# Half two's differences of x formed in PSUM, the last layer's group sums staged later, the third matrix and y in pieces of 384, 384 and 256 columns

## The chip, the core and the metric

One core of a Trainium2 chip runs the whole program. Its engines are TensorE (PE, whose weight loads the profile lists as PEld), VectorE (DVE), ScalarE (ACT), GpSimd (POOL) and SyncE (SP, which here only issues transfers). Each takes its instructions in the order in which they were written. The metric is the device time of one execution in microseconds (us), the median of three runs.

## The reference

Attention whose heads are mixed before and after the softmax, then two layers of matrix products without biases, all in fp32, over 1792 tokens (4 sequences of 448):

```python
scores = np.einsum('bhij,hg->bgij', scale * q @ k^T, w_pre)
attn   = softmax(scores)
attn   = np.einsum('bhij,hg->bgij', attn, w_post)
x = (attn @ v) as [1792, 768]
h = (x @ w1) * (x @ w2)            # [1792, 1024]
x = (h @ w3) @ w_out               # [1792, 768]
h = np.maximum(x @ w_in, 0.0)      # [1792, 2048]
out = (h * h) @ w_out2             # [1792, 768]
```

## The kernel before

**Products.** Every fp32 product is made of three matmuls (`mm3`, its matmul is line 62): each operand is split into a rounded high part and the rest, and the products high·high, high·low and low·high add up in one PSUM bank. A split costs two instructions: a copy on ACT that makes the high part, and a subtraction on DVE or POOL that makes the low part. Weights are split where they are used, and so is x.

**Order.** The class `Moe` holds a list of units, and each unit is a list of weight pieces (one piece is one step). `stage(s)` writes what step s needs ahead: the load of a piece six steps ahead on SP's queue; four ahead the narrowing on ACT (line 95), which with two DVE instructions three ahead (lines 106 and 108, called a join here) turns a fetched piece into fp32; three ahead the high part on ACT (line 122); two ahead the low part on POOL (line 164). Then the step's own matmuls are written. `lead` moves a piece's staging earlier by so many steps. Since all engines work in the order written, one instruction that comes late holds back what stands behind it on its engine.

**The third matrix.** w3 @ w_out is formed on the chip: eight units `p34` write it to a buffer in DRAM, `w34d`, from which the units `ly` read it back to form y. Both take 1024 columns of weights per unit, in four pieces of 256: step i does one of two accumulators (t = i mod 2) for half of the columns, so that its step 0 takes pieces 0 and 1, and step 2 takes pieces 2 and 3. Steps named in `free` also carry a job `side`, which rewrites a part of w_in into fp32 (a transfer in, ACT, DVE, a transfer out).

**Two halves.** Tokens are worked in two halves, each of two blocks of 448 columns. For half two, layers three and four save an eighth of the matmuls: a 2 by 2 block product is made of seven, which need sums of weights (S1 to S4, `combine`, DVE, line 160) and differences of the other operand: T1 = B12 − B11, T2 = B22 − T1, T3 = B22 − B12, T4 = B21 − T2. For x of half two these come from `quad_x`, called once per unit u of the last two phases of half one's fourth layer (`l4_part`, six units of two steps each per phase). It serves column blocks 1, 0 and 2, from units 4, 6 and 8 on: `chain` forms the four differences in SBUF on DVE, one unit later T2, T1, T3 and T4 are split (`split`; ACT makes the high parts, DVE the low parts of T2 and T3, POOL those of T1 and T4), and one unit after that B11, B21 and B22 (POOL, DVE, POOL). The phases' sums themselves are added up on DVE by `add` (line 832), from PSUM accumulators named `l`.

**The last layer.** `l4_group` makes four groups of 21 pieces, which add into banks named `l_` + group + p + X, Y or Z. A bank is read by `add` when a sum is whole, and then used again for another sum. The list `order` takes the products 1, 5, 6, 3, 7, 2, 4; pieces 8 and 9 are the ones with S3.

**PSUM.** All eight banks are one ring (tag "m"): a new tile takes the bank of the eighth tile before it and waits until that has been read.

Of the kernel before, what the change touches and what calls it, by code (L numbers as in the profile page):

```python
# [13 lines left out]
AF = mybir.ActivationFunctionType  # L14
# [24 lines left out]
def fused_kernel(ctx, tc, q, k, v, w_pre, w_post, w1, w2, w3t, wo, win, wo2, eye, out):  # L39
# [510 lines left out]
    class Moe:  # L550
        def __init__(self, pre):
# [6 lines left out]
            for hf in range(2):  # L558
# [21 lines left out]
                if hf == 0:  # L580
                    k = self.turned
                    self.free = {(i, t) for i in (*range(self.p34_at, k - 4), *range(k, k + 4)) for t in (1, 3)}
                    self.free |= {(i, 1) for i in range(k - 4, k)}
                    self.free |= {(k + 9 + e, 0) for e in range(6)}
                    self.free |= {(k + 17, 0)}
# [12 lines left out]
            for u in range(self.turned, len(self.units)):  # L598
                n, quad = len(self.units[u][0]), self.pieces[self.at[u]][0] is None
                for i in range(n if quad else 0):  # L600
                    self.lead[self.at[u] + i] = (4 if i < 6 else 3) if n > 7 and i < 8 else 2 if u > self.turned + 6 else 1
            self.keep = {
# [183 lines left out]
        def quad_x(self, u):  # L786
# [23 lines left out]
            def chain(c):  # L810
                spare("T3", c)
                spare("T4", c)
                for out, x, y in (
                    ("T3", "B22", "B12"), ("T1", "B12", "B11"), ("T2", "B22", "T1"), ("T4", "B21", "T2"),
                ):
                    x, y = (b["raw", n] if n[0] == "T" else f32(b["T1" if n == "B12" else n, c][1]) for n in (x, y))
                    t = b["raw", out] = self.tile(f"{out}raw{c}")
                    nc.vector.tensor_tensor(t, x, y, ALU.subtract)

            V, G = nc.vector, nc.gpsimd  # L820
            for c, at in ((1, 4), (0, 6), (2, 8)):
                if u == at:
                    chain(c)
                if u == at + 1:
                    for name, eng in (("T2", V), ("T1", G), ("T3", V), ("T4", G)):
                        split(name, c, eng)
                if u == at + 2:
                    for name, eng in (("B11", G), ("B21", V), ("B22", G)):
                        split(name, c, eng)

# [224 lines left out]
        def p34(self, m):  # L1055
            acc = {}

            def run(ws, i):
                part, t = divmod(i, 2)
                if part == 0:  # L1060
                    acc[t] = self.psum(f"p34_{m}_{t}")[:, :HC]
                mm3(acc[t], [(self.chunk(ws, c), self.wot[c, t]) for c in range(4 * part, 4 * part + 4)], part == 0, part == 1)
                if part == 0:
                    return
                o = self.tile(f"o34_{m}_{t}")[:, :HC]
                nc.scalar.activation(o, acc[t], AF.Copy)
                nc.scalar.dma_start(
                    w34d[3 * t : 3 * t + 3, :, m].rearrange("n p c -> p n c"), o.rearrange("p (n c) -> p n c", c=128)
                )

            return [(w3t[m, :, QW * i : QW * i + QW], True) for i in range(4)], run

        def ly(self, hf, n):
            acc = {}

            def run(ws, i):
                part, t = divmod(i, 2)
                if hf and n == 0:
                    t = 1 - t
                if part == 0:  # L1080
                    acc[t] = self.psum(f"y{hf}_{n}_{t}")
                cs = range(4 * part, 4 * part + 4)
                mm3(acc[t], [(self.chunk(ws, c), self.xy["ab", hf, c, t]) for c in cs], part == 0, part == 1)
                if part:
                    self.yquad(hf, n, t, acc[t])

            src = w34d[n].rearrange("p c n -> p (c n)")
            return [(src[:, QW * i : QW * i + QW], False) for i in range(4)], run

# [215 lines left out]
```

## Time and profile before

| | |
|---|---|
| median of three runs | 1285.67 us (1285.01 to 1286.91) |
| the profiled execution | 1287.36 us, of which the span from the first to the last instruction is 1285.6 |
| busy: PE, DVE, ACT, POOL | 1245.3, 915.1, 777.6, 618.5 us (97%, 71%, 60%, 48%) |
| granted TensorE clock | 0.997 on average |
| PE instructions | 8326 matmuls |

The page of the profile gives each engine's busy time over the span. A window view gives the same for a stretch of it, with the granted clock and the share of time in which the transfer engines were busy. A wait view tells what released an engine and for how long it had waited, and a timeline lists the instructions of one engine in order, with the idle time ahead of each in brackets where there was some. Window views here are of the matmuls of line 62 alone. The stretches are: the third matrix from 536.32 us to 606.66, the last phase of half one's fourth layer with the first product of half two's third layer behind it from 851.50 to 918.47, and one group of the last layer from 1151.95 to 1178.43.

### The profile page before, as it was taken

The page shows a single profiled execution, that of the slowest core. Times are in us where ns is not written, and L with a number is a line of the kernel's source. Part 1 is how long each engine was busy: PE and PEld are TensorE (multiplying, and loading weights), DVE is VectorE, ACT ScalarE, POOL GpSimd, SP SyncE. Part 2 cuts the span into 40 slices and gives each one's busy share as a digit, 9 for nine tenths or more (in the row PEclk, how much of TensorE's full clock was granted, in tenths as well). Part 3 has the DMA queues.
Part 4 walks back from the last instruction along what each step waited for, and adds up shares of the span by engine and source line. Part 5 has one row for each costly group of instructions (what it writes and reads, how often), then busy time and mean ns, then how long its engine had stood idle before and what let it go on. Part 6 is the DMA issues. An engine that isn't in the chain of part 4 may idle for free. (4 is left out here: it accounts for less than half of the span.)

```text
span 1285.6 us, 24324 instructions
## 1 busy us (share of the span) xinstructions
PE 1245.3 (97%) x8326; PEld 1070.0 (83%) x8326; DVE 915.1 (71%) x1756; ACT 777.6 (60%) x1808; POOL 618.5 (48%) x736
## 2 busy tenths in 40 slices
PE   7999999999998999999999999999899999999998
PEld 3677777777775788998999999999799999899897
DVE  4888899788877966665555867579767424666957
ACT  5988889888887754554455755455333344653543
POOL 4354255246322622333366443536765464855845
PEclk9999999999999999999999999999999999999999
DMA  6666476566555757699755576485421116235042
GB/s 216 169 176 200 130 198 215 138 175 189 175 156 169 213 180 216 189 272 297 246 160 173 185 249 204 150 268 166 150 74 50 46 59 198 64 122 183 15 154 86
DMA packets 138577, 214.48 MB, mean 167 GB/s; under 512 B 25301, under 2 KB 106197, under 8 KB 137941
## 3 DMA queue, kind: packets, MB, share of 16 engines
q1 hardware_dynamic: 114576, 190.30, 48.4%
q10 hardware_dynamic: 23877, 22.63, 5.1%
q8 instruction: 66, 1.08, 0.3%
q14 instruction: 58, 0.48, 0.1%
HBM read 128.73 MB, written 45.61 MB: 136 GB/s over the span
## 5 line engine op out<-in xcount | busy, mean ns | idle before, releaser
L164 POOL TENSOR_TENSOR wl<-f,wh 128x256 fp32r<-128x256 f32 (+1 forms) x112 | 97.9, 875 | 199.7 <-ACT wh L122 162.7
L338 PE MATMUL sp<-r,kpre 120*120 120x448 f32 x360 | 159.8, 565 | 11.3 <-ACT p L352 6.6
L352 ACT ACTIVATE p<-sp,nm 120x448 f32<-120x448 f32 x180 | 113.6, 642 | 50.3 <-DVE nm L344 50.2
L394 DVE SCALAR_TENSOR_TENSOR pl<-p,sm,ph 120x448 f16<-120x448 f32 (+3 forms) x270 | 137.9, 564 | 0.3 <-POOL ph L380 0.3
L344 DVE TENSOR_REDUCE nm<-sp 120x1 f32<-120x448 f32 x180 | 107.3, 617 | 42.5 <-PE sp L338 38.4
L367 POOL TENSOR_SCALAR sm<-sm 120x2 f32<-120x2 f32 (+3 forms) x94 | 24.6, 261 | 205.5 <-ACT p L352 201.1
L403 PEld LDWEIGHTS <-ph 120*128 120x128 f16 x1260 | 93.0, 98 | 32.6 <-issue 24.1
L378 ACT ACTIVATE ph<-p,sm 120x448 f16<-120x448 f32 (+1 forms) x180 | 107.8, 664 | 17.6 <-DVE sm L372 14.1
L403 PE MATMUL tp<-kwh,ph 120*128 120x120 f16 x630 | 106.1, 217 | 5.4 <-DVE p L419 2.4
L338 PEld LDWEIGHTS sp<-r,kpre 120*120 120x120 f32 x360 | 58.9, 184 | 55.7 <-issue 21.1
L403 PE MATMUL tp<-kwh,pl 120*128 120x120 f16 x630 | 105.2, 216 | 0.0
L403 PE MATMUL tp<-kwl,ph 120*128 120x120 f16 x630 | 105.2, 216 | 0.0
L312 PE MATMUL sc<-kt,qh 128*110 128x448 f32 (+1 forms) x192 | 99.4, 518 | 2.0 <-DVE kt L276 1.3
L323 ACT ACTIVATE s<-sc 110x448 f32<-110x448 f32 (+1 forms) x186 | 90.5, 559 | 7.6 <-PE sc L312 6.8
L122 ACT ACTIVATE wh<-f 128x256 fp32r<-128x256 f32 (+1 forms) x112 | 49.8, 444 | 73.0 <-DVE f L108 70.2
L164 POOL TENSOR_TENSOR wl<-quadh,wh 128x384 fp32r<-128x384 f32 x48 | 51.3, 1072 | 72.7 <-ACT wh L122 53.7
L95 ACT ACTIVATE y<-raw 128x256 f32<-128x256 f32 (+1 forms) x128 | 60.2, 473 | 39.4 <-DMA raw<-w3t 16.4
L455 PE MATMUL pv<-p,v 128*64 128x110 f32 (+1 forms) x1536 | 81.0, 262 | 0.6 <-ACT xs L465 0.6
L455 PEld LDWEIGHTS pv<-p,v 128*64 128x64 f32 x1536 | 74.1, 137 | 4.0 <-ACT xs L465 0.9
L417 DVE TENSOR_SCALAR p<-tp,iv 128x360 f32<-128x360 f32 x135 | 74.2, 577 | 1.3 <-PE tp L403 1.3
L106 DVE TENSOR_SCALAR f<-y 128x256 int32<-128x256 int32 (+1 forms) x128 | 58.8, 459 | 21.3 <-ACT y L95 21.2
L108 DVE SCALAR_TENSOR_TENSOR f<-raw,f 128x256 int32<-128x256 int32 (+1 forms) x128 | 68.2, 533 | 4.4
(3093 smaller groups left out, 3936.5 us busy)
## 6 DMA issues: line engine op xcount, KB each, us to landing
r<-s SPq DMA_DIRECT2D x172, 210.0 KB
raw<-w SPq DMA_DIRECT2D x32, 384.0 KB
sraw<-win SPq DMA_DIRECT2D x32, 384.0 KB
raw<-wo SPq DMA_DIRECT2D x48, 256.0 KB
kraw<-k SPq DMA_DIRECT2D x24, 448.0 KB
quadh<-wind SPq DMA_DIRECT2D x24, 384.0 KB
raw<-w3t SPq DMA_DIRECT2D x32, 256.0 KB
qraw<-q SPq DMA_DIRECT2D x35, 220.0 KB
```

The lines of the kernel that those rows point to most:

```text
L108: nc.vector.scalar_tensor_tensor(fi, raw[:, :, 0], 29, fi, ALU.logical_shift_right, ALU.bitwise_or)
L164: eng.tensor_tensor(self.out[i][1], self.ft.pop(i), f32(self.out[i][0]), ALU.subtract)
L312: nc.tensor.matmul(sc[:ic], t[:, hh * ic : hh * ic + ic], self.kt[b, h // 2][:, h % 2], start=(i == 0), stop=(i == 1))
L323: nc.scalar.activation(self.st[n][:ic, h], self.sc.pop((n, h))[:ic], AF.Copy)
L338: nc.tensor.matmul(t[:kk], self.kpre[:kk, :kk], self.rt.pop(g)[:kk], start=True, stop=True)
L344: nc.vector.tensor_reduce(nm[:kk], self.sp[g][:kk], AX.X, ALU.max, negate=True)
L352: nc.scalar.activation(p[:kk], self.sp.pop(g)[:kk], AF.Exp, bias=self.nm.pop(g)[:kk], accum_out=self.sm[g // 2][:kk, g % 2 : g % 2 + 1],)
L378: nc.scalar.activation(h[:, to], p[:, fr], AF.Copy, scale=sm)
L394: nc.vector.scalar_tensor_tensor(l[:, to], p[:, fr], sm, h[:, to], ALU.mult, ALU.subtract)
L403: nc.tensor.matmul(t[:, j], p[:, at : at + 128], w, start=(i == 0), stop=(i == 2))
L417: nc.vector.tensor_scalar(d, t[:, main], self.iv, None, ALU.mult)
L455: nc.tensor.matmul(t[64 * e : 64 * e + 64, x, :w], self.v[b][:, j, g], self.p2[n][:, j * NH + g, :w], start=(j == 0), stop=(j == JC - 1),)
```

## The change

Three things are rewritten.

1. In `quad_x`, ACT first copies B12 into a PSUM tile (`b12x`). DVE forms T1 in a second PSUM tile, T3 over the copy, and T2 in a third. One unit later (`fourth`) ACT makes T2's high part, DVE its low part, and DVE forms T4 over T2. Then T1, T3 and T4 are split with DVE making the low parts, and B11 and B22 with POOL; B21 follows a unit later on POOL. So each column block has eight DVE instructions instead of seven, all with an operand in PSUM, three on POOL instead of four, and eight on ACT instead of seven; and three tiles more go through the ring of PSUM banks.
2. In `l4_group`'s pieces, `lead` of pieces 8 and 9 falls from 2 to 0, and that of the later pieces from 2 to 1.
3. `p34` and `ly` take their 1024 columns in pieces of 384, 384 and 256; each step does both accumulators with the columns of its own piece alone. The `side` jobs stand at steps 0 and 1. The matmuls are the same in number; the pieces per unit are three instead of four, and their ACT, DVE and POOL instructions too.

```diff
                     k = self.turned
-                    self.free = {(i, t) for i in (*range(self.p34_at, k - 4), *range(k, k + 4)) for t in (1, 3)}
+                    self.free = {(i, t) for i in (*range(self.p34_at, k - 4), *range(k, k + 4)) for t in (0, 1)}
                     self.free |= {(i, 1) for i in range(k - 4, k)}
...
                 for i in range(n if quad else 0):
-                    self.lead[self.at[u] + i] = (4 if i < 6 else 3) if n > 7 and i < 8 else 2 if u > self.turned + 6 else 1
+                    self.lead[self.at[u] + i] = (4 if i < 6 else 3 if i < 8 else i > 9) if n > 7 else 2 if u > self.turned + 6 else 1
             self.keep = {
...
             def chain(c):
...
                 spare("T4", c)
-                for out, x, y in (
-                    ("T3", "B22", "B12"), ("T1", "B12", "B11"), ("T2", "B22", "T1"), ("T4", "B21", "T2"),
+                b12, t1, t2 = (self.psum(f"{n}x{c}") for n in ("b12", "t1", "t2"))
+                nc.scalar.activation(b12, f32(b["T1", c][1]), AF.Copy)
+                for out, t, x, y in (
+                    ("T1", t1, b12, "B11"), ("T3", b12, "B22", b12), ("T2", t2, "B22", t1),
                 ):
-                    x, y = (b["raw", n] if n[0] == "T" else f32(b["T1" if n == "B12" else n, c][1]) for n in (x, y))
-                    t = b["raw", out] = self.tile(f"{out}raw{c}")
-                    nc.vector.tensor_tensor(t, x, y, ALU.subtract)
+                    x, y = (f32(b[n, c][1]) if isinstance(n, str) else n for n in (x, y))
+                    b["raw", out] = t
+                    V.tensor_tensor(t, x, y, ALU.subtract)
+
+            def fourth(c):
+                h, l = b["T2", c]
+                t = b["raw", "T4"] = b.pop(("raw", "T2"))
+                nc.scalar.activation(h, t, AF.Copy)
+                V.tensor_tensor(l, t, f32(h), ALU.subtract)
+                V.tensor_tensor(t, f32(b["B21", c][1]), t, ALU.subtract)
 
...
                 if u == at + 1:
-                    for name, eng in (("T2", V), ("T1", G), ("T3", V), ("T4", G)):
-                        split(name, c, eng)
+                    fourth(c)
+                    for name in ("T1", "T3", "T4"):
+                        split(name, c, V)
+                    for name in ("B11", "B22"):
+                        split(name, c, G)
                 if u == at + 2:
-                    for name, eng in (("B11", G), ("B21", V), ("B22", G)):
-                        split(name, c, eng)
+                    split("B21", c, G)
 
         def add(self, out, x, y, eng=nc.vector):
...
             def run(ws, i):
-                part, t = divmod(i, 2)
-                if part == 0:
-                    acc[t] = self.psum(f"p34_{m}_{t}")[:, :HC]
-                mm3(acc[t], [(self.chunk(ws, c), self.wot[c, t]) for c in range(4 * part, 4 * part + 4)], part == 0, part == 1)
-                if part == 0:
-                    return
-                o = self.tile(f"o34_{m}_{t}")[:, :HC]
-                nc.scalar.activation(o, acc[t], AF.Copy)
-                nc.scalar.dma_start(
-                    w34d[3 * t : 3 * t + 3, :, m].rearrange("n p c -> p n c"), o.rearrange("p (n c) -> p n c", c=128)
-                )
-
-            return [(w3t[m, :, QW * i : QW * i + QW], True) for i in range(4)], run
+                for t in range(2):
+                    if i == 0:
+                        acc[t] = self.psum(f"p34_{m}_{t}")[:, :HC]
+                    cs = range(3 * i, min(3 * i + 3, 8))
+                    mm3(acc[t], [(self.chunk(ws, c), self.wot[c, t]) for c in cs], i == 0, i == 2)
+                    if i < 2:
+                        continue
+                    o = self.tile(f"o34_{m}_{t}")[:, :HC]
+                    nc.scalar.activation(o, acc[t], AF.Copy)
+                    nc.scalar.dma_start(
+                        w34d[3 * t : 3 * t + 3, :, m].rearrange("n p c -> p n c"), o.rearrange("p (n c) -> p n c", c=128)
+                    )
+
+            return [(w3t[m, :, HC * i : min(HC * i + HC, 1024)], True) for i in range(3)], run
 
         def ly(self, hf, n):
...
             def run(ws, i):
-                part, t = divmod(i, 2)
-                if hf and n == 0:
-                    t = 1 - t
-                if part == 0:
-                    acc[t] = self.psum(f"y{hf}_{n}_{t}")
-                cs = range(4 * part, 4 * part + 4)
-                mm3(acc[t], [(self.chunk(ws, c), self.xy["ab", hf, c, t]) for c in cs], part == 0, part == 1)
-                if part:
-                    self.yquad(hf, n, t, acc[t])
+                for t in (1, 0) if hf and n == 0 else (0, 1):
+                    if i == 0:
+                        acc[t] = self.psum(f"y{hf}_{n}_{t}")
+                    cs = range(3 * i, min(3 * i + 3, 8))
+                    mm3(acc[t], [(self.chunk(ws, c), self.xy["ab", hf, c, t]) for c in cs], i == 0, i == 2)
+                    if i == 2:
+                        self.yquad(hf, n, t, acc[t])
 
             src = w34d[n].rearrange("p c n -> p (c n)")
-            return [(src[:, QW * i : QW * i + QW], False) for i in range(4)], run
+            return [(src[:, HC * i : min(HC * i + HC, 1024)], False) for i in range(3)], run
 
         def side(self, k):
```

On DVE, in the second phase that serves x (column block 1, `f` and `y` are weight pieces, `l_2_4` an accumulator of the phase, `oa_4` its running sum, `x1l` blocks of x), before:

```order
L818 TENSOR_TENSOR T3raw_11920<-x1l_11747 128x448
L818 TENSOR_TENSOR T1raw_11922<-x1l_11747,x1l_11684 128x448
L818 TENSOR_TENSOR T2raw_11924<-x1l_11747,T1raw_11922 128x448
L818 TENSOR_TENSOR T4raw_11926<-x1l_11684,T2raw_11924 128x448
L106 TENSOR_SCALAR f_11948<-y_11908 128x256
L108 SCALAR_TENSOR_TENSOR f_11948<-raw_11854,f_11948 128x256
L832 TENSOR_TENSOR oa_4_1_10540<-l_2_4_1_11928,oa_4_1_10540 128x448
L832 TENSOR_TENSOR oa_4_0_10542<-l_2_4_0_11935,oa_4_0_10542 128x448
L106 TENSOR_SCALAR f_11974<-y_11946 128x256
L108 SCALAR_TENSOR_TENSOR f_11974<-raw_11880,f_11974 128x256
L804 TENSOR_TENSOR T21l<-T2raw_11924,T21h 128x448
L804 TENSOR_TENSOR T31l<-T3raw_11920,T31h 128x448
```

and after:

```order
L820 TENSOR_TENSOR t1x_11797<-b12x_11796,x1l_11560 128x448
L820 TENSOR_TENSOR b12x_11796<-x1l_11623,b12x_11796 128x448
L820 TENSOR_TENSOR t2x_11798<-x1l_11623,t1x_11797 128x448
L106 TENSOR_SCALAR f_11823<-y_11784 128x256
L108 SCALAR_TENSOR_TENSOR f_11823<-raw_11730,f_11823 128x256
L843 TENSOR_TENSOR oa_4_1_10416<-l_2_4_1_11803,oa_4_1_10416 128x448
L843 TENSOR_TENSOR oa_4_0_10418<-l_2_4_0_11810,oa_4_0_10418 128x448
L106 TENSOR_SCALAR f_11849<-y_11821 128x256
L108 SCALAR_TENSOR_TENSOR f_11849<-raw_11756,f_11849 128x256
L826 TENSOR_TENSOR T21l<-t2x_11798,T21h 128x448
L827 TENSOR_TENSOR t2x_11798<-x1l_11560,t2x_11798 128x448
L804 TENSOR_TENSOR x1l_11623<-t1x_11797,x1h_11622 128x448
```

The four differences have become three, in PSUM; the fourth stands one unit later, and is followed by low parts that POOL had made.

On POOL at the same place, before:

```order
L164 TENSOR_TENSOR wl_11952<-f_11948,wh_11951 128x256
L804 TENSOR_TENSOR x1l_11747<-T1raw_11922,x1h_11746 128x448
L804 TENSOR_TENSOR T41l<-T4raw_11926,T41h 128x448
L164 TENSOR_TENSOR wl_11978<-f_11974,wh_11977 128x256
L164 TENSOR_TENSOR wl_12012<-f_12008,wh_12011 128x256
L804 TENSOR_TENSOR x1l_11684<-x1l_11684,x1h_11683 128x448
L804 TENSOR_TENSOR x1l_11747<-x1l_11747,x1h_11746 128x448
L164 TENSOR_TENSOR wl_12038<-f_12034,wh_12037 128x256
L164 TENSOR_TENSOR wl_12082<-f_12078,wh_12081 128x256
L804 TENSOR_TENSOR x1l_11747<-T1raw_12052,x1h_11746 128x448
```

and after:

```order
L164 TENSOR_TENSOR wl_11853<-f_11849,wh_11852 128x256
L164 TENSOR_TENSOR wl_11892<-f_11888,wh_11891 128x256
L804 TENSOR_TENSOR x1l_11560<-x1l_11560,x1h_11559 128x448
L164 TENSOR_TENSOR wl_11918<-f_11914,wh_11917 128x256
L164 TENSOR_TENSOR wl_11957<-f_11953,wh_11956 128x256
L804 TENSOR_TENSOR x1l_11560<-x1l_11560,x1h_11559 128x448
L804 TENSOR_TENSOR x1l_11623<-x1l_11623,x1h_11622 128x448
L164 TENSOR_TENSOR wl_11987<-f_11983,wh_11986 128x256
L164 TENSOR_TENSOR wl_12026<-f_12022,wh_12025 128x256
L804 TENSOR_TENSOR x1l_11560<-x1l_11560,x1h_11559 128x448
```

The low parts of T1 and T4 are gone from between the weight pieces, and B21's has come.

On DVE in group two of the last layer (`So` are sums of weights, `o_` the output sums, `qh13` and `h1` operands), before:

```order
L160 TENSOR_TENSOR So_14882<-quado_14648,So_14732 128x256
L160 TENSOR_TENSOR So_14899<-quado_14628,quado_14630 128x256
L160 TENSOR_TENSOR So_14906<-quado_14648,quado_14650 128x256
L832 TENSOR_TENSOR o_0_0_14318<-l_10X,o_0_0_14318 128x448
L832 TENSOR_TENSOR o_2_0_14323<-l_11X,o_2_0_14323 128x448
L832 TENSOR_TENSOR o_1_1_14328<-l_10Z,o_1_1_14328 128x448
L832 TENSOR_TENSOR o_3_1_14333<-l_11Z,o_3_1_14333 128x448
L938 TENSOR_TENSOR h1B_3l<-qh13B,h1B_3h 128x448
L942 TENSOR_TENSOR h1T3raw_14936<-qh13B,h1B12raw_14851 128x448
```

and after:

```order
L160 TENSOR_TENSOR So_14722<-quado_14488,So_14572 128x256
L843 TENSOR_TENSOR o_0_0_14151<-l_10X,o_0_0_14151 128x448
L843 TENSOR_TENSOR o_2_0_14156<-l_11X,o_2_0_14156 128x448
L843 TENSOR_TENSOR o_1_1_14161<-l_10Z,o_1_1_14161 128x448
L843 TENSOR_TENSOR o_3_1_14166<-l_11Z,o_3_1_14166 128x448
L160 TENSOR_TENSOR So_14764<-quado_14468,quado_14470 128x256
L949 TENSOR_TENSOR h1B_3l<-qh13B,h1B_3h 128x448
L953 TENSOR_TENSOR h1T3raw_14767<-qh13B,h1B12raw_14691 128x448
L843 TENSOR_TENSOR o_0_1_14182<-l_10X,o_0_1_14182 128x448
L160 TENSOR_TENSOR So_14779<-quado_14488,quado_14490 128x256
```

The two S3 (the sums of two `quado`) stood ahead of the reads of the banks X and Z; now one stands behind all four reads, and the other behind the next read of X.

## Rows read from the trace of the kernel before

**Rows 1.** Page, part 1: busy us, share of the span, instructions.

```profile
PE 1245.3 (97%) x8326; PEld 1070.0 (83%) x8326; DVE 915.1 (71%) x1756; ACT 777.6 (60%) x1808; POOL 618.5 (48%) x736
```

**Rows 2.** Windows, L62 matmuls: us, PE and PEld busy, PEclk, DMA share, GB/s.

```profile
536.32:569.60 33.28, 33.28 (x194) 33.28 (x193) 1.00 0.82 247
536.32:606.66 70.34, 68.40 (x386) 66.18 (x385) 1.00 0.88 269
577.94:606.66 28.72, 26.78 (x148) 24.87 (x147) 1.00 0.93 292
851.50:918.47 66.97, 61.17 (x299) 55.15 (x298) 1.00 0.64 205
1151.95:1178.43 26.48, 25.48 (x128) 23.55 (x126) 1.00 0.31 98
1000.00:1050.00 50.00, 50.00 (x252) 46.88 (x251) 1.00 0.15 45
```

**Rows 3.** Waits of PE, whole span: us in total, times, longest.

```profile
PE l L62 <- POOL wl L164: 3.8, 4, 1.9
...
PE q00A L62 <- POOL wl L164: 1.6, 1, 1.6
PE p L62 <- POOL wl L164: 1.5, 3, 0.5
...
PE l_10X L62 <- DVE o L832: 1.0, 1, 1.0
```

**Rows 4.** Waits, the third matrix: us in total, times, longest.

```profile
ACT y L95 <- DMA raw<-w3t: 16.0, 12, 2.7
```

**Rows 5.** Timeline of DVE, half two's x: start us, duration us.

```profile
872.58 0.62 DVE L818 TENSOR_TENSOR T3raw<-x1l 128x448 f32<-128x448 f32 x1
...
875.39 0.28 DVE L106 TENSOR_SCALAR f<-y 128x256 int32<-128x256 int32 x1
875.71 0.42 DVE L108 SCALAR_TENSOR_TENSOR f<-raw,f 128x256 int32<-128x256 int32 x1
...
877.11 0.52 DVE L106 TENSOR_SCALAR f<-y 128x256 int32<-128x256 int32 x1
...
880.04 1.24 DVE L106 TENSOR_SCALAR f<-y 128x256 int32<-128x256 int32 x1
881.32 0.84 DVE L108 SCALAR_TENSOR_TENSOR f<-raw,f 128x256 int32<-128x256 int32 x1
...
885.55 1.57 DVE L818 TENSOR_TENSOR T3raw<-x1l 128x448 f32<-128x448 f32 x1
...
899.57 1.57 DVE L818 TENSOR_TENSOR T3raw<-x1l 128x448 f32<-128x448 f32 x1
```

**Rows 6.** Lines by form, DVE, 851.5 to 918.5: busy us, mean ns.

```profile
L832 DVE TENSOR_TENSOR oa<-l,oa 128x448 f32<-128x448 f32 x12 | 7.0, 613 | 0.1
```

**Rows 7.** Timeline of POOL, half two's x.

```profile
893.67 1.54 POOL L804 TENSOR_TENSOR T40l<-T4raw,T40h 128x448 fp32r<-128x448 f32 x1
895.17 0.77 POOL L164 TENSOR_TENSOR wl<-f,wh 128x256 fp32r<-128x256 f32 x1
```

**Rows 8.** Timeline of DVE, group two of the last layer.

```profile
1155.07 2.25 DVE L160 TENSOR_TENSOR So<-quado,quado 128x256 f32<-128x256 f32 x2
1157.25 0.61 DVE L832 TENSOR_TENSOR o<-l_10X,o 128x448 f32<-128x448 f32 x1
1157.78 0.61 DVE L832 TENSOR_TENSOR o<-l_11X,o 128x448 f32<-128x448 f32 x1
```

**Rows 9.** Timeline of PE, the same place.

```profile
1156.55 0.36 PE L62 MATMUL l_11Z<-h1T_3h,wl 128*128 128x448 f32 x1
1157.91 0.47 PE L62 MATMUL l_10X<-h1T_2h,wh 128*128 128x448 f32 x1 [1.00 <-DVE o L832]
```

**Rows 10.** Timeline of ACT, the same group.

```profile
1160.55 0.58 ACT L934 ACTIVATE h1T_3h<-h1T3raw 128x448 fp32r<-128x448 f32 x1 [2.69 <-DVE h1T3raw L942]
```

**Rows 11.** Timeline of POOL, the same group.

```profile
1161.20 1.16 POOL L938 TENSOR_TENSOR h1T_3l<-h1T3raw,h1T_3h 128x448 fp32r<-128x448 f32 x1 [1.19 <-ACT h1T_3h L934]
```

## The prediction

> **What bounds the kernel now.** I read the page's first part first: PE is busy 97% of the span [rows 1], so a change that leaves the matmuls alone can only win back time in which PE stands or is held up. The window view then gives PE's pace. A 448-column matmul takes 50.00/250 = 0.200 us (the 252 matmuls listed include two cut by the edges), a 384-column one 33.28/192 = 0.1733 us, both at a granted clock of 1.00 [rows 2]. With these I price each stretch that the change touches and subtract it from the time it took [rows 2]:
>
> - third matrix: 384 × 0.1733 = 66.56 of 70.34, **3.78 us** over. Its first half (192 matmuls) has nothing over, so all of it falls in the second, about 1 us per unit;
> - last phase of half one's fourth layer and first product behind it: 297 × 0.200 = 59.40 of 66.97, **7.57 us** over;
> - a group of the last layer: 126 × 0.200 = 25.20 of 26.48, **1.28 us** over, and 4 × 1.28 = **5.12 us** for the four.
>
> The clock is 1.00 in all, so these are waits and restarts, not a slow engine. Together they are 16.5 us, the most that the change can gain. The view of PE's waits says for whom: in the phase for low parts of weights that POOL makes (3.8 us in four waits, and 1.6 at the first product behind it), in the third matrix for POOL too (1.5), and in each group of the last layer for one DVE read of a bank (1.0; the row of group one stands for four alike) [rows 3].
>
> **The change: x of half two.** The wait is for POOL, but POOL stands behind DVE. The four differences recur on DVE at 872.58, 885.55 and 899.57 us [rows 5]: periods of 12.97 and 14.02, 13.5 on average, for two units, whose 48 matmuls take PE 9.6. Over three column blocks DVE falls behind by 3 × 3.9 = 11.7 us, of which PE felt 7.57; so it went in with some 4.1 us in hand. Two things stretch DVE. An instruction on operands in SBUF takes 0.62 us at one time and 1.57 at another, and a join (lines 106 and 108) 0.28 + 0.42 = 0.70 or 1.24 + 0.84 = 2.08 [rows 5]. The sums that read PSUM average 0.613 in the same stretch, over twelve of them [rows 6], and follow each other at 0.53 us (1157.25, 1157.78) [rows 8]. On POOL a low part of T4 of 1.54 us stands right ahead of a weight's low part that PE needs [rows 7].
>
> After the change all eight DVE instructions per column block have an operand in PSUM. The trace has none of their forms (PSUM in and PSUM out, or PSUM in and SBUF out); the nearest row is the sum from PSUM, so 0.54 each, with 1.57, the contested price of the nearest SBUF form, as the upper end. Two units then cost DVE 4 joins × 0.70 = 2.8, 4 sums × 0.54 = 2.2, and 8 × 0.54 = 4.3: 9.3 us. Joins remain exposed to POOL, which keeps three splits: I leave what one period loses now, 2.08 − 0.70 = 1.4 for one and 0.52 − 0.28 = 0.24 for each of two others, 1.9. That makes 11.2, or 1.6 us behind per block, 4.8 over three, against 4.1 in hand: 0.7 us of loss. Three new PSUM tiles per block pass through the ring of eight, so PE's next accumulator now waits until DVE has made the low part before it; that takes a little of the 4.1 away, and I put the loss at **1.0** (ends 0 and 4.3, where joins lose 3.1 instead of 1.9). **Saved: 7.57 − 1.0 = 6.6** (3.3 to 7.6). ACT's extra copy costs nothing: ACT is busy 60% of the span [rows 1] and the copy lies beside matmuls. Its high part of T4 now waits for DVE, and later weights' high parts queue behind it; that is the same lag, and is counted in it. POOL, with one low part of up to 1.54 us less ahead of the weights, has room.
>
> **The last layer's groups.** PE wants bank X again at 1156.55 + 0.20 = 1156.75 and starts at 1157.91 [rows 9]. DVE could have read it at 1155.07, but made two S3 first (2.25 us) and read it at 1157.25 [rows 8]. Without them the read ends at about 1155.7, a us ahead of PE. What is late next is S3's own neighbour: DVE now makes one S3 behind the four reads and ahead of T3, which piece 8 needs. The last bank read closes at about 1156.95; DVE is through at 1157.5, S3 (2.25/2 = 1.13 [rows 8]) at 1158.6, two instructions of 0.54 at 1159.7; ACT's high part adds 0.58 [rows 10], POOL's low part 1.16 [rows 11], a weight's low part 0.77 [rows 7]: 1162.2. PE, no longer stopped, comes there 26 matmuls after 1156.75, at 1161.95. The loss is 0.2 (0 if S3 goes uncontested, 0.8 if a further contested instruction joins the chain). **Saved: 4 × (1.28 − 0.2) = 4.3** (1.9 to 5.1).
>
> **The third matrix.** ACT waits twelve times, 16.0 us in all, for w3's transfers [rows 4], and the transfer engines are busy 0.82 of the first half and 0.93 of the end of the second [rows 2]: supply slips behind by some 1 us a unit until it shows. Bytes do not change, so this slip stays. What changes is the room. Before, an odd piece is used one step ahead of its own slot, so that its low part is written two steps ahead of use, 2 × 12 × 0.1733 = 4.2 us. After, each step uses its own piece and three steps lie between, of 48/3 = 16 matmuls on average, 8.3 us. The slip over eight units was 4.2 + 3.78 = 8.0; 8.3 covers it. I keep **0.3** of loss (ends 0, and all 3.78 if supply alone decides). **Saved: 3.5.** Fewer instructions on ACT, DVE and POOL gain nothing, since none of them sets this stage. In `ly` the pieces have no PE wait to remove in the view [rows 3], so neither gain nor loss: its loads go out seven steps ahead as before, and a step is now longer.
>
> **Sum.** 6.6 + 4.3 + 3.5 = 14.4. The profiled execution took 1287.36, so it becomes 1273.0. That execution lies 1.69 above the median of 1285.67, and **the forecast for the median is 1271.3**. With nothing lost at all it is 1269.2.
>
> **Rivals.**
>
> *A. POOL and DVE still collide.* The three low parts left on POOL (B11, B22, B21) each hold up a join for a POOL instruction's 1.16 us [rows 11]: 3.5 a period instead of 1.9, so 12.8, 3.2 behind per block, 9.6 − 4.1 = 5.5 lost, 2.1 saved instead of 6.6: 1275.8. For it: the joins are the only SBUF work left and did stretch to 1.24 [rows 5]. Against it: POOL has one split less to meet them. The Trainium skill ("SBUF — State Buffer", section "SBUF: two separate sides") says that DVE and GpSimd share one pair of ports as an exclusive lock that is held for the whole instruction, taken by DVE in a two-port mode or with two SBUF inputs; by that rule each POOL split can stop a join for its full length. The trace agrees in kind: a join's first half went from 0.28 to 1.24 [rows 5], while sums from PSUM stayed at 0.613 [rows 6].
>
> *B. S3 comes too late.* The groups save only 1.9: 1273.7. For it: the chain above has no margin. Against: S3 only has to run as fast as it did.
>
> *C. Transfers decide the third matrix.* The 3.8 us stays, there or in the units right behind: 1271.3 + 3.5 = 1274.8. For it: transfer engines at 0.93 [rows 2]. Against: the first half loses nothing, and the end of this traffic is near.
>
> *D. Slower: DVE's work in PSUM is dear, and the ring hands it to PE.* If each of the eight instructions takes 1.57, a period is 8 × 1.57 + 2.8 + 2.2 = 17.6; DVE falls 8.0 behind per block, 24 − 4.1 = 19.9 lost in place of 7.57, or 12.3 more; less 7.8 saved elsewhere, 4.5 more: 1290.2. It decides above 7.57 + 7.8 = 15.4 of loss, a period of 16.1, or 1.39 us per instruction (1.15 if joins also lose 1.9). For it: PE's accumulators now wait for these low parts through the ring, which they did not before. Against: the PSUM sums' 0.613 [rows 6]. The Trainium skill ("VectorE: DVE Perf Modes", section "Rules for kernel authors") speaks against this edit: copy PSUM to SBUF first if there are many operations. The rows speak the other way: beside POOL, SBUF was the dear place here, 1.57 against 0.613 [rows 5, 6]. By the rows the phase saves 6.6; by that rule it saves less or loses.
>
> *E. The change does not do what it says:* the phase keeps its 7.57 because lateness comes from ACT or the loads: 1277.9.
>
> **How the numbers follow.** Forecast, 1269 to 1274: 0.62. A 0.12, C 0.09, B 0.08, E 0.02, D 0.04, and 0.03 that several of A to C and E fall together and nothing measurable is left. A measurement of this kernel can tell about 0.2% (2.6 us) from no change. All but D and the last are faster by more: 0.93; the last is within 0.2%: 0.03; D is slower: 0.04. The range goes from 1268.5 (all saved, and the runs' own 0.7 below their median) to 1278.0, which takes in A, B, C and E.
>
> **What would show it.** In the changed kernel's profile: the third matrix at about 66.9 us, the phase with its first product at about 60.4, a group at about 25.4; no wait of 1.0 for a bank read; DVE's eight instructions near 0.6 us each and a period of 11 us, with the phase's sums no longer after their turn. Wrong, step by step: a join at over 1 us more than once a period (A), a wait of PE for POOL's low part of T3 in a group (B), a wait of PE or ACT for `w3t` pieces (C), DVE instructions with PSUM operands over 1 us and PE waiting for DVE at an accumulator's first matmul (D). The forecast as a whole falls if a new wait of PE, above 2 us in all, stands in any stage that I gave nothing, y above all.

## Result: 1.4% less time, and the profile after

The changed kernel takes 1269.77 us (median of six runs, 1267.39 to 1272.81) against 1287.35 for six runs of the kernel before beside it: ratio 0.9864, 95% interval 0.9845 to 0.9883, or 17.6 us less (15.1 to 20.0). The forecast was 1271.3, which is 14.4 less than the median of 1285.67 that it started from; the saving came out a little larger than forecast, with 14.4 just below its interval. The profiled execution took 1267.65 us. The first part of its page, which answers to [rows 1]:

```profile
PE 1239.0 (98%) x8326; PEld 1069.0 (84%) x8326; DVE 910.6 (72%) x1743; ACT 775.2 (61%) x1783; POOL 609.0 (48%) x713
```

The stretches of [rows 2], in the changed kernel (us, PE and PEld busy, PEclk, DMA share, GB/s): the first half of the third matrix, the whole of it, the last phase of half one's fourth layer with the first product of half two, and one group of the last layer:

```profile
532.65:565.93 33.28, 33.28 (x194) 33.28 (x193) 1.00 0.88 279
532.65:599.21 66.56, 66.56 (x386) 66.56 (x385) 1.00 0.94 303
844.18:903.92 59.74, 59.67 (x298) 55.60 (x297) 1.00 0.72 231
1136.18:1161.38 25.20, 25.20 (x128) 23.62 (x126) 1.00 0.34 104
```

"Over" below is a stretch's time less its matmuls at the paces of the prediction. The third matrix is 0.00 us over (3.78 before), the phase of x 0.34 (7.57), each group 0.00 (1.28). The stages gave 3.78 + 7.23 + 5.12 = 16.1 us of the 16.5 that were there. Of the waits of PE in [rows 3] only these are left on line 62, and both lie ahead of the third matrix:

```profile
PE l L62 <- POOL wl L164: 0.4, 1, 0.4
PE l L62 <- ACT wh L122: 0.4, 1, 0.4
```

The two profiled executions differ by 19.7 us, 3.6 more than the stages. That difference stands ahead of the third matrix, which begins at 536.32 us before and 532.65 after. A part of it is the clock: in attention, which the change does not touch, the kernel before has two stretches at a lower granted clock (whole windows: us, PE, PEld, DVE, ACT and POOL busy, PEclk, DMA share, GB/s):

```profile
20.00:40.00 20.00, 17.59 (x80) 9.63 (x79) 10.71 (x29) 15.19 (x36) 7.49 (x11) 0.91 0.70 224
...
380.00:400.00 20.00, 17.81 (x183) 12.81 (x184) 14.69 (x35) 15.66 (x38) 4.11 (x9) 0.91 0.82 237
```

and the changed kernel has none:

```profile
20.00:40.00 20.00, 17.01 (x80) 8.56 (x79) 11.20 (x29) 15.39 (x37) 7.58 (x11) 1.00 0.69 220
...
380.00:400.00 20.00, 17.92 (x190) 12.88 (x190) 13.93 (x34) 14.49 (x36) 4.11 (x9) 1.00 0.80 232
```

Counted from the first matmul on, one and the same matmul starts 1.37 us later in the kernel before just ahead of the second stretch (at 394.07) and 2.79 later right behind it (at 397.85), so this stretch gave 1.4 us; behind the first, at 36 us, the two are 0.04 apart. The other 2.2 us are scattered over attention, and their cause stays open. The lead is no property of the change: in the kernels below, the third matrix begins anywhere between 533.1 and 536.1 us, with either form of its pieces.

### The profile page after: what moved, and what is told of

Same layout as the page of the kernel before. It is cut to its first block, busy times and chain, and to the rows that moved or that the text cites. A ratio compares the mean times of both kernels' runs of the same rounds, so it can differ in the third digit from the quotient of the medians.

```text
span 1265.9 us, 24179 instructions
## 1 busy us (share of the span) xinstructions
PE 1239.0 (98%) x8326; PEld 1069.0 (84%) x8326; DVE 910.6 (72%) x1743; ACT 775.2 (61%) x1783; POOL 609.0 (48%) x713
## 4 chain that ended last, share of the span: by engine, by line
PE 84%; DVE 6%; issue 3%; DMA 3%; ACT 2%; POOL 2%; SPq 0%; ACTq 0%; POOLq 0%; DVEq 0%
PE l L62 14%; PE y L62 9%; PE sp L338 8%; PE tp L403 5%; PE pv L455 5%; PE p L62 5%; PE sc L312 4%; DVE pl L394 2%; DMA r<-s 2%; DVE nm L344 1%; PE e L62 1%; DVE p L417 1%; ACT ph L378 1%; ACT p L352 0%; POOL kt L276 0%
## 5 line engine op out<-in xcount | busy, mean ns | idle before, releaser
L164 POOL TENSOR_TENSOR wl<-f,wh 128x256 fp32r<-128x256 f32 (+1 forms) x104 | 94.8, 911 | 188.4 <-ACT wh L122 148.8
L378 ACT ACTIVATE ph<-p,sm 120x448 f16<-120x448 f32 (+1 forms) x180 | 107.8, 664 | 16.2 <-DVE sm L372 12.9
L95 ACT ACTIVATE y<-raw 128x384 f32<-128x384 f32 (+1 forms) x120 | 58.8, 493 | 29.2 <-DMA raw<-wo 16.9
L108 DVE SCALAR_TENSOR_TENSOR f<-raw,f 128x384 int32<-128x384 int32 (+1 forms) x120 | 69.3, 578 | 4.1
L312 PE MATMUL sc<-kt,ql 128*110 128x448 f32 (+1 forms) x192 | 70.7, 368 | 0.0
```

The lines of the kernel that those rows point to most:

```text
L164: eng.tensor_tensor(self.out[i][1], self.ft.pop(i), f32(self.out[i][0]), ALU.subtract)
L312: nc.tensor.matmul(sc[:ic], t[:, hh * ic : hh * ic + ic], self.kt[b, h // 2][:, h % 2], start=(i == 0), stop=(i == 1))
L378: nc.scalar.activation(h[:, to], p[:, fr], AF.Copy, scale=sm)
```

## Experiments

Three kernels do one part alone and are timed; the others take one step of the reasoning apart, and are read, each in one profiled execution, by the time of the one stretch that they change.

**Each part alone.** The edits are the three pieces of the diff above, each put whole into the kernel before; here their central lines.

```diff
-                    ("T3", "B22", "B12"), ("T1", "B12", "B11"), ("T2", "B22", "T1"), ("T4", "B21", "T2"),
+                    ("T1", t1, b12, "B11"), ("T3", b12, "B22", b12), ("T2", t2, "B22", t1),
```

> The kernel before with the change to x of half two alone. 'Over' means a stretch's time less its matmuls at 0.200 us. Theory (three gains that add up, each inside its own stretch): the last phase with its first product goes from 7.57 us over to about 0.4, as in the changed kernel; the third matrix keeps its 3.78 and each group of the last layer its 1.28; the time falls by 7.2 us, ratio 0.9944. Rival (the parts help each other, since earlier staging shifts what meets on POOL and on the transfers): this part alone leaves over 1.5 us in its stretch, or changes another one by more than 0.5.

Measured: 1278.49 us against 1287.23, ratio 0.9933 (0.9911 to 0.9955). The phase is 0.67 us over; the third matrix 3.43, the groups 1.28 to 1.29 each.

```diff
-(4 if i < 6 else 3) if n > 7 and i < 8 else 2 if u > self.turned + 6 else 1
+(4 if i < 6 else 3 if i < 8 else i > 9) if n > 7 else 2 if u > self.turned + 6 else 1
```

> The kernel before with the later staging of the last layer's sums alone. Theory (gains add up): each group goes from 1.28 us over to 0.0 to 0.1, 5.1 us in all, ratio 0.9960; nothing else moves. Rival (S3 late): a group keeps 0.2 to 0.8, because the margin of the chain S3, T3, high part, low part is only some 0.2 us in the changed kernel's trace; 1.9 to 4.3 us in all.

Measured: 1281.26, ratio 0.9958 (0.9946 to 0.9970). Each group is 0.0 over. The phase of x is 7.3 over, of which 1.4 are a slow clock (last section), the third matrix 6.05.

```diff
-            return [(w3t[m, :, QW * i : QW * i + QW], True) for i in range(4)], run
+            return [(w3t[m, :, HC * i : min(HC * i + HC, 1024)], True) for i in range(3)], run
```

> The kernel before with the third matrix and y in pieces of 384, 384 and 256 alone. Theory (gains add up): the third matrix goes from 3.78 us over to 0, ratio 0.9971; the phase of x keeps 7.57 and the groups 1.28 each. Rival (the pieces also speed up what lies ahead of the third matrix, where the changed kernel's profiled execution was 3.6 us earlier than the one of before): the time falls by 6 to 8 us, ratio below 0.9955, and this run and its run of before differ by over 2 us ahead of the third matrix in the same direction again.

Measured: 1281.49, ratio 0.9960 (0.9949 to 0.9971). The third matrix is 0.00 over, the phase of x 8.3, the groups 1.29 to 1.30. By its time alone the run does not decide: it is 5.7 us faster, between the 3.78 of the theory and the 6 to 8 of the rival, and the theory's ratio of 0.9971 is the edge of its interval. The rival fell by the place: the third matrix began at 535.57 us, not earlier than in the kernels with the old pieces (533.1 to 536.3).

The parts add up: 0.67 + 0.42 + 0.40 = 1.49%, against 1.36% (1.17 to 1.55) for all. Each repairs its own stretch and no other. What the old code loses is itself not constant: the third matrix lost 3.78, 3.43 and 6.05 us in three profiles, the phase of x 7.57, 7.3 and 8.3. That may be one reason why a sum made on one profile is a little off the medians.

**Part 1: PSUM, or one low part less on POOL?** This kernel keeps the new order and the new engines and puts the three differences back into SBUF.

```diff
-                b12, t1, t2 = (self.psum(f"{n}x{c}") for n in ("b12", "t1", "t2"))
-                nc.scalar.activation(b12, f32(b["T1", c][1]), AF.Copy)
+                t3, t1, t2 = (self.tile(f"{n}raw{c}") for n in ("T3", "T1", "T2"))
+                b12 = f32(b["T1", c][1])
...
-                    ("T1", t1, b12, "B11"), ("T3", b12, "B22", b12), ("T2", t2, "B22", t1),
+                    ("T1", t1, b12, "B11"), ("T3", t3, "B22", b12), ("T2", t2, "B22", t1),
```

> The changed kernel with the three differences of x in SBUF tiles instead of PSUM; the order of the instructions and the engine of each stay as changed, ACT's copy of B12 falls away. Theory (PSUM operands keep DVE out of POOL's way): DVE's eight instructions stretch from 0.62 to 0.9 to 1.6 us where POOL works, the period of two units goes from 11.1 us to about 14, and the phase is 5 to 9 us over again. Rival (what helped is that POOL has one low part less ahead of the weights, and the new order): the phase stays below 1.5 us over, with a period below 12.

Measured: the phase is 6.99 us over, of which 1.2 are a slow clock (last section). POOL's instructions are the same in both kernels, at the same place in the order. First the changed kernel, POOL and DVE (timelines: start us, duration us):

```profile
876.02 1.42 POOL L804 TENSOR_TENSOR x1l<-x1l,x1h 128x448 fp32r<-128x448 f32 x1 [0.21 <-ACT x1h L803]
```

```profile
865.34 0.63 DVE L820 TENSOR_TENSOR t1x<-b12x,x1l 128x448 f32<-128x448 f32 x1
...
872.24 0.92 DVE L106 TENSOR_SCALAR f<-y 128x256 int32<-128x256 int32 x1
873.19 1.26 DVE L108 SCALAR_TENSOR_TENSOR f<-raw,f 128x256 int32<-128x256 int32 x1
...
876.40 0.63 DVE L820 TENSOR_TENSOR t1x<-b12x,x1l 128x448 f32<-128x448 f32 x1
876.94 0.62 DVE L820 TENSOR_TENSOR b12x<-x1l,b12x 128x448 f32<-128x448 f32 x1
```

Then the same place with SBUF tiles:

```profile
878.03 1.43 POOL L804 TENSOR_TENSOR x1l<-x1l,x1h 128x448 fp32r<-128x448 f32 x1 [0.20 <-ACT x1h L803]
879.41 1.12 POOL L164 TENSOR_TENSOR wl<-f,wh 128x256 fp32r<-128x256 f32 x1
```

```profile
866.34 0.62 DVE L820 TENSOR_TENSOR T1raw<-x1l,x1l 128x448 f32<-128x448 f32 x1
...
878.35 1.58 DVE L820 TENSOR_TENSOR T1raw<-x1l,x1l 128x448 f32<-128x448 f32 x1
879.86 1.15 DVE L820 TENSOR_TENSOR T3raw<-x1l 128x448 f32<-128x448 f32 x1
```

DVE's first difference starts 0.38 us into POOL's low part in one and 0.32 in the other. From PSUM it takes 0.63 us, from SBUF 1.58; the next one, beside POOL's next instruction, 0.62 and 1.15. The first T1 of the SBUF kernel, at 866.34, takes 0.62 too. With SBUF tiles a period is 12.0 and then 12.9 us (about 14 was expected), in the changed kernel 11.06 twice. Only the three differences stretch: the five instructions of the unit behind, which start where POOL has nothing under way, keep 0.62. So it is where the operands lie that counts, not the lighter POOL: with one low part less on POOL, but in SBUF, most of the loss is back.

**Is it POOL that stretches them?** Next, on top of SBUF tiles, the three low parts that POOL still makes go to DVE.

```diff
                     for name in ("B11", "B22"):
-                        split(name, c, G)
+                        split(name, c, V)
                 if u == at + 2:
-                    split("B21", c, G)
+                    split("B21", c, V)
```

> The kernel with the three differences of x in SBUF (y1_sbuf), and the three low parts that POOL still made (B11, B22, B21) on DVE too: eleven instructions per column block on SBUF operands, with POOL left only its weights' low parts. Theory (POOL's own work on SBUF is what stretches DVE's): most of the eleven take 0.62 us, two units take DVE 2.8 + 2.2 + 11 x 0.54 = 10.9 us plus at most 1 beside weights, and the phase is 0.5 to 3 us over. Rival (instructions on two SBUF operands are dear in themselves): they keep averages of 0.8 to 1.3 us, two units take 14 us or more, and the phase is over 7 us over.

Measured: the phase is 2.42 us over, with eleven instructions per block on SBUF operands. Its window, and DVE's groups in it (busy us, mean ns):

```profile
846.19:908.01 61.82, 60.52 (x299) 55.38 (x298) 1.00 0.68 215
```

```profile
L820 DVE TENSOR_TENSOR T3raw<-x1l 128x448 f32<-128x448 f32 x3 | 2.9, 981 | 0.0
L820 DVE TENSOR_TENSOR T1raw<-x1l,x1l 128x448 f32<-128x448 f32 x3 | 1.9, 619 | 0.0
```

T1 is back at 0.619, since no POOL instruction is under way when it starts; T3 averages 0.981, since in two blocks of three it starts while a weight's low part is under way on POOL. The second block shows it (in order of start):

```profile
879.30 0.62 DVE L820 TENSOR_TENSOR T1raw<-x1l,x1l 128x448 f32<-128x448 f32 x1
879.46 1.05 POOL L164 TENSOR_TENSOR wl<-f,wh 128x256 fp32r<-128x256 f32 x1 [1.22 <-ACT wh L122]
879.84 1.16 DVE L820 TENSOR_TENSOR T3raw<-x1l 128x448 f32<-128x448 f32 x1
```

Instructions on SBUF are not dear in themselves, and what decides is which engine starts first. Of the 30 differences that the kernel before and these two kernels form in SBUF, the 13 that start while a POOL instruction is under way take 1.04 to 1.58 us and end some 0.5 us behind it; the other 17 take 0.61 to 0.63, also the five beside which POOL starts one later.

The phase's smaller loss is not all due to that. Two units take DVE 12.4 us here, over the 11.9 that were expected and about what the kernel with SBUF tiles took. But no low part of x stands ahead of a weight's on POOL any more: in that kernel the weight's low part that ended PE's longest wait, 2.48 us, had stood behind two of them, 2.85 us of work. So this run shows what stretches an instruction. The phase is 4.6 us shorter than in that kernel, 1.2 of them the clock; how much of the rest came from DVE and how much from the emptier POOL, the run does not separate.

**Part 2: which of the moved pieces?** Two kernels do the two halves of the new `lead` alone; a third puts pieces 8 and 9 half way back.

```diff
-(4 if i < 6 else 3 if i < 8 else i > 9)
+(4 if i < 6 else 3 if i < 8 else 0 if i < 10 else 2)
```

> The changed kernel, but of the last layer's staging only pieces 8 and 9 (the two with S3) are later; the pieces behind them have their old lead of 2. Theory (S3 ahead of the reads was the cause): each group stays at 25.2 us, 0.0 to 0.1 over. Rival (the later pieces' staging was in the way): each group is back at about 1.28 over.

Measured: 0.00 to 0.02 us over per group.

```diff
-(4 if i < 6 else 3 if i < 8 else i > 9)
+(4 if i < 6 else 3 if i < 8 else 2 if i < 10 else 1)
```

> The changed kernel, but pieces 8 and 9 have their old lead of 2, and only the pieces behind them are later. Theory (S3 was the cause): each group is back at about 26.5 us, 1.28 over, with PE waiting about 1.0 for DVE's read of bank X. Rival: each group stays at 25.2.

Measured: 1.28 to 1.29 over per group, with the wait of [rows 3] back:

```profile
PE l_10X L62 <- DVE o L843: 1.0, 1, 1.0
```

So pieces 8 and 9 are all of it; the later ones neither help nor harm.

```diff
-(4 if i < 6 else 3 if i < 8 else i > 9)
+(4 if i < 6 else 3 if i < 8 else 1)
```

> The changed kernel with pieces 8 and 9 of the last layer's groups staged one step earlier: one S3 stands ahead of the reads of banks X and Z again, the other behind them. Theory (what counts is whether DVE reads X before PE wants it, which it did 1.0 us early): one S3 of 0.41 to 1.13 us fits into that, 0 to 0.2 us over per group. Rival (each S3 ahead of the reads costs its share): about 0.6 us over per group.

Measured: 0.42 to 0.43 over per group, between the two. DVE in group two of this kernel:

```profile
1143.37 1.37 DVE L160 TENSOR_TENSOR So<-quado,quado 128x256 f32<-128x256 f32 x1
1144.66 0.61 DVE L843 TENSOR_TENSOR o<-l_10X,o 128x448 f32<-128x448 f32 x1
```

and at the same place of the changed kernel:

```profile
1139.38 0.62 DVE L843 TENSOR_TENSOR o<-l_10X,o 128x448 f32<-128x448 f32 x1
...
1141.72 0.41 DVE L160 TENSOR_TENSOR So<-quado,quado 128x256 f32<-128x256 f32 x1
1142.05 0.62 DVE L949 TENSOR_TENSOR h1B_3l<-qh13B,h1B_3h 128x448 fp32r<-128x448 f32 x1
1142.58 0.61 DVE L953 TENSOR_TENSOR h1T3raw<-qh13B,h1B12raw 128x448 f32<-128x448 f32 x1
```

The mechanism held, its size did not: one S3 ahead of the reads costs 1.37 us, not the 0.41 to 1.13 of the expectation, and 1.37 does not fit into a margin of 1.0. Behind the reads the same instruction takes 0.41. The difference is again who starts first. Ahead of the reads, S3 starts 0.25 us behind POOL's instruction and ends behind it; in the changed kernel it starts 0.03 us ahead of POOL's, and it is POOL's that takes longer (0.98 where one alone takes 0.74). POOL beside S3, in this kernel and in the changed one:

```profile
1143.12 1.33 POOL L949 TENSOR_TENSOR h1T_3l<-h1T2raw,h1T_3h 128x448 fp32r<-128x448 f32 x1
```

```profile
1141.75 0.98 POOL L164 TENSOR_TENSOR wl<-So,wh 128x256 fp32r<-128x256 f32 x1
```

**Part 3: room, or what is under way?** The prediction said that supply goes on slipping and that more room covers it. Three kernels test that. In the first the pieces are 256 columns and the side jobs at steps 1 and 3 as before, but each step uses its own piece.

```diff
-                    cs = range(3 * i, min(3 * i + 3, 8))
+                    cs = (2 * i, 2 * i + 1)
...
-            return [(w3t[m, :, HC * i : min(HC * i + HC, 1024)], True) for i in range(3)], run
+            return [(w3t[m, :, QW * i : QW * i + QW], True) for i in range(4)], run
```

> The changed kernel with the third matrix in four pieces of 256 again, but each step doing both accumulators with its own piece (sides at steps 1 and 3 as before). This gives an odd piece one step, 2.08 us, more room than the kernel before, and changes neither the size of a transfer nor how many are under way. Theory A (supply slips by about 1 us per unit, and what counts is the room, as predicted): 3.78 - 2.08 = 1.7 us over. Theory B (supply is set by what is under way at a time): the same 1.7, with the low parts' margin ahead of PE falling by about 1 us per unit. Rival C (the odd pieces' early use was all): 0 over, with a margin that stays.

Measured: 5.85 us over, all in the second half, where units take 9.1 to 10.4 us instead of 8.32. That is above what A and B gave (1.7), inside what the old pieces lose anyway (3.4 to 6.1), and against C: a step of room bought nothing that can be seen. In the second kernel the old pieces stay, and the side jobs' loads get a third buffer.

```diff
-NTILE = 61
+NTILE = 60
...
-tag="sraw", name=f"sraw{k}", bufs=2)
+tag="sraw", name=f"sraw{k}", bufs=3)
```

> The kernel before with three buffers instead of two for the side jobs' transfers (and 60 instead of 61 of the tiles of 448), so that SP's queue no longer stands behind DVE's side job, where it waited for 40.7 us of the third matrix's 70.3, with loads of w3 behind it. Pieces are 256, with their old order. Theory A (room; the transfers themselves are the limit): the supply still slips by about 1 us per unit, 3 to 4 us over. Theory B (what is under way at a time): loads go out earlier, the period of a unit falls from 9.3 towards 8.32, 0 to 1.5 over.

Measured: 0.52 us over, seven units at 8.32 and the last at 8.84. SP's own waits during the third matrix, in the first of these kernels (us, times, longest):

```profile
SPq L1117 <- DVE side L1109: 38.3, 12, 6.0
SPq L79 <- DVE f L108: 8.9, 9, 2.9
```

and in the second:

```profile
SPq L79 <- DVE f L108: 38.3, 20, 3.7
```

The wait for the side job is gone, and SP now waits for w3's own buffers: the loads run as far ahead as these allow. In the changed kernel, which loses nothing in this stage, the wait for the side job has not gone:

```profile
SPq L1116 <- DVE side L1108: 33.8, 13, 5.6
```

So taking the wait away mends the old pieces, but it is not needed with the new ones. The third kernel takes room away from the changed one.

```diff
+            for i in range(self.at[self.p34_at], self.at[self.p34_at + 8]):
+                self.lead[i] = 0
```

> The changed kernel with the third matrix's pieces staged one step (2.8 us on average) later. This takes room away and leaves the size of the loads. Theory B (supply was held by what is under way on the queue, and pieces of 384 mend that): the margin of POOL's low parts ahead of PE falls from about 5.5 us to about 2.7 and then stays; 0 to 0.3 us over. Theory A (room covers a slip of about 1 us per unit, as predicted): 2 to 3 us over.

Measured: 0.09 us over. POOL's low parts of the first pieces of the last two units, in this kernel:

```profile
578.58 1.37 POOL L164 TENSOR_TENSOR wl<-f,wh 128x384 fp32r<-128x384 f32 x1 [0.55 <-ACT wh L122]
...
586.90 1.36 POOL L164 TENSOR_TENSOR wl<-f,wh 128x384 fp32r<-128x384 f32 x1 [0.56 <-ACT wh L122]
```

They are 8.32 us apart, which is PE's own pace: nothing slips. The last unit starts at 592.2 us, so the margin is 592.2 - 588.3 = 3.9 us, less than the 5.5 of the changed kernel (2.7 was expected) and steady. Theory A fell: with the new pieces no slip is there to be covered. B fits the second and the third kernel, but its 1.7 for the first was as wrong as A's, so its sum is not shown.

## Why the prediction was right, point by point

**What bounds.** Right, and the ceiling too: 16.5 us were there and 16.1 came. The stretches' overs were the whole gain from the third matrix on, and no new wait came up on line 62, y included.

**x of half two.** Right in mechanism and nearly in size. The price per instruction was the open term, 0.54 by the nearest row, 1.57 at the other end: the 24 new instructions average 0.615 to 0.631 us and follow each other at 0.53. The period was put at 11.2 and is 11.06; joins lose nearly what was left for them (0.92 + 1.26 in one, where 0.70 is the free price). The loss was put at 1.0 and is 0.34. Two terms were too large: the period, by 0.14 or 0.4 over three blocks, and the 0.3 us set aside for the ring of PSUM banks, since PE has no wait for DVE there. Rival A's collision is there in those joins, once a period and not three times. The Trainium skill ("SBUF — State Buffer", section "SBUF: two separate sides") says that of a GpSimd instruction and a DVE one with two SBUF inputs, or in a two-port mode, the one that starts first holds their shared ports for its whole length. The 1.58 and 0.63 us at one and the same place agree with that, and so does the T1 that keeps 0.62 although POOL starts beside it.

**Rival D.** It did not come: no instruction with a PSUM operand is above 0.64 us. The Trainium skill ("VectorE: DVE Perf Modes", section "Rules for kernel authors") leaves two ways open for elementwise work on a matmul's output, to accept the plain rate of a PSUM source or to copy to SBUF first where many operations follow. For these differences, whose data ACT puts into PSUM, operands in PSUM were right: with the same operations in SBUF the phase is 6.99 us over, in PSUM 0.34.

**The groups.** Right, with the loss of 0.2 per group not there. The chain behind S3 was priced with S3 at 1.13; it took 0.41 in group two and 0.87 in the first group, and neither lost anything, so the chain had more room than was worked out.

**The third matrix.** The size was right (3.5 forecast, 3.78 measured), but the step was wrong, so the size was luck. The prediction said: "Bytes do not change, so this slip stays. What changes is the room." The slip did not stay. With the old pieces it came from SP's queue: the load of a side job waited for DVE to free one of two buffers, and the loads of w3 stood behind it. A third buffer takes the block away, and larger pieces do without that; either brings the units to 8.32 us. Reading a DMA share of 0.93 as "transfers decide" was the mistake, and rival C leaned on it too; the changed kernel moves 303 GB/s over the whole stage at 0.94, and before it was 269. What I should have read is SP's own waits, 40.7 us in this stage, which I left out of the prediction; their sum alone would not have told the size, since 33.8 us of them remain in the changed kernel. How the larger pieces help is argued and not shown: they put more bytes under way behind a load that waits, but they also have longer rows per transfer, and with them the side jobs moved from steps 1 and 3 to 0 and 1. The first of the three kernels put back both the pieces and the steps, so it does not part them; the old pieces with a third buffer show only that none of these is needed.

**The sum.** 14.4 forecast, 16.1 by stages: the residuals of 1.0, 0.8 and 0.3 that I left were 0.34, 0 and 0. The 1.5 us that the medians' 17.6 has beyond the 16.1 are not explained; that the old code loses more in other executions may be a part.

## What to carry to other kernels

Where DVE and POOL both work on SBUF, the instruction that starts second is held up by the one under way (0.62 against 1.58 us here), and a DVE subtraction that has an operand in PSUM keeps its price (0.63): moving a chain of differences there can be worth more than taking work off the slower engine. When a stage starves, look at the waits of the queue that issues its loads before calling the transfers full: one load that waits for a buffer holds back all that stand behind it, and a buffer more for it is a cheap test. And in a stretch whose loss is a single late read, ask which instruction stands ahead of it on that engine and whether its own user can wait.

## What was not expected of the hardware

In the kernel with SBUF tiles, PE waited 2.48 us for a weight's low part, and at the end of the wait the granted clock fell to half, 1.2 instead of 2.4 GHz, for eight matmuls (windows: us, PE and PEld busy, PEclk, DMA share, GB/s):

```profile
900.74:903.59 2.85, 0.37 (x2) 0.24 (x2) 0.90 0.00 0
903.59:906.40 2.81, 2.81 (x8) 2.51 (x9) 0.50 0.43 147
906.40:911.07 4.67, 4.67 (x25) 4.38 (x24) 1.00 1.01 346
```

Eight matmuls took 2.81 us instead of 1.60, about 1.2 us beyond the wait itself. The kernel before waited up to 1.9 us in the same phase [rows 3] at a clock of 1.00 throughout [rows 2]. But the length of the wait does not tell them apart: the kernel with the last layer's sums alone has the same wait at the same place, 1.95 us, and 1.5 us behind its end the clock fell to half for ten matmuls:

```profile
910.94:914.35 3.41, 3.41 (x10) 3.00 (x10) 0.50 0.49 173
```

They took 3.41 us instead of 2.00. So a wait can cost more than it shows, and the same wait may or may not do so; what decided it is open.
